# Chunked attention and a gated feed-forward: attention products in quarters of the array, two groups at a time

## The chip, the cores and the metric

The kernel runs on one core of one Trainium2 chip. A core has TensorE (PE in the profile, its weight loads PEld), VectorE (DVE), ScalarE (ACT), GpSimd (POOL, used here to issue loads that cast to bf16) and SyncE (SP, used here to issue transposing copies and the stores). The metric is the device time of one execution in microseconds. Before the change it is 248.89 us, the median of 3 runs (248.65 to 249.34).

## The reference, cut to what matters

q, k and v have 8 batches, 8 heads, 576 positions and 64 features, in float32. Attention stays within chunks of 64 positions, nine of them to a sequence. The result, 4608 tokens of 512 features, goes through a gated feed-forward.

```python
chunk = 64
q_c = q.reshape(B, H, nc, chunk, D)            # and k_c, v_c
scores = scale * np.matmul(q_c, k_c.transpose(0, 1, 2, 4, 3))
scores = scores - np.max(scores, axis=-1, keepdims=True)
attn = np.exp(scores)
attn = attn / (np.sum(attn, axis=-1, keepdims=True) + 1e-09)
out = np.matmul(attn, v_c).reshape(B, H, S, D)

x = out.transpose(0, 2, 1, 3).reshape(B * S, H * D)     # 4608 x 512
a, b = x @ w1, x @ w2                                   # 512 x 1024 each
h = a * b @ w3                                          # w3 1024 x 1024
return h @ w_out                                        # w_out 1024 x 512
```

## The kernel before, in words

**Groups and tiles.** A group is two chunks of all eight heads, 128 tokens; there are 36. Four groups make a tile of 512 tokens for the feed-forward, nine tiles in all. The kernel first forms w3 times w_out once (`add_w3o`: for each of eight rows of w3, 8 transposes, a copy, 8 products against w_out, a copy), so that a tile needs only `a` and `b` (64 products of 128x512, line 589), a multiplication `abT` on DVE (line 598), and 32 products against `w3o_sb` (line 620). `a` is copied out of PSUM by ACT first (`a_sb`).

**A group's attention** (`add_group`). q and k come as `raw` with tokens on the partitions. They are turned: groups 4 to 11 by PE (line 418, 8 transposes into a `ffn` buffer of PSUM, then copies), groups 12 to 35 by a transposing DMA on SP's queue into `kqT` (line 422). The scores of a pair of heads in one product need the two heads apart: q is copied into `qd`, a tile that is zero outside its two diagonal blocks (`q_copy`, two copies of 64 partitions), so that one product of full depth 128 and full width 128 gives 128x64 scores. Eight such products fill `p_sc` (line 447). Then DVE takes the maximum (line 452) and subtracts it (460), ACT takes the exponential (464), DVE sums, inverts and multiplies (468 to 474). The probabilities `an` are turned into `at`, for groups 0 to 15 by PE (line 479) and for the others by a DMA (line 428). Eight products against the padded v, `vd`, fill `p_av` (line 490); one copy takes that to `xt`, from which the feed-forward reads. `vd` and `qd` are zeroed at the start (lines 250 to 264).

**The first tile** is different: two "quads" (`load_quad`, `quad_turn`) bring q and k of four groups with rows of four tokens, 1 KB in DRAM, and PE turns 64 columns at a time, the two heads of a pair into the two halves of the partitions (line 380). Scores, values and copies undo the order of the tokens (lines 398, 405, 457).

**What sets the order.** Every step is added to a plan with the engines that it may run on, a cost, a key (the smaller the earlier), what it follows, and the buffers that it takes and reads. `Plan.run` plays this through and gives each engine a fixed order of instructions. Loads are issued by POOL in the order of the list `LOADS`, then group by group; the weights w1, w2, w3 and half of w_out, q, k and v all come by this one queue. The other half of w_out is staged by SP and ACT at the start (line 350). Stores start after the last load of q and k has come. Until the first product that takes `p_av`, PE's waits are filled with products on zeros (line 683).

**PSUM** has eight banks: six `ffn` buffers, one `p_sc`, one `p_av`. Scores hold theirs until DVE has subtracted the maximum, values until the copy to `xt` has been made.

Of the kernel before, what the change touches and what calls it, by code (L numbers as in the profile page):

```python
# [30 lines left out]
FLOWN, QUEUED, LAG = 3.5, 3.4, 1.2  # L31
# [143 lines left out]
def kernel(  # L175
# [21 lines left out]
    C = 64  # L197
# [16 lines left out]
    BUFS = {"raw": 6, "rawq": 2, "kqT": 4, "kT": 3, "qd": 3, "vd": 3, "sd": 2, "e": 2, "an": 4, "at": 6, "w3t": 2, "abT": 2,  # L214
            "a_sb": 3, "o_sb": 18, "xt": XT, "ffn": 6, "p_sc": 1, "p_av": 1}
# [19 lines left out]

    qds = [wpool.tile([P, 2, NM, 2 * C], bf, tag=f"qd{i}", name=f"qd{i}") for i in range(BUFS["qd"])]
    vds = [wpool.tile([P, NM, NCH, 2 * D], bf, tag=f"vd{i}", name=f"vd{i}") for i in range(BUFS["vd"])]
    rawqs = [wpool.tile([P, 2, 2, 2, R * D], bf, tag=f"rawq{i}", name=f"rawq{i}") for i in range(BUFS["rawq"])]
# [3 lines left out]
    plan = Plan(BUFS, ("qd", "kT", "kqT", "p_sc", "sd", "e", "an", "at", "p_av", "xt"))  # L242

    def copy(eng, o, i):
        if eng == "ACT":
            nc.scalar.copy(o, i)  # L246
        else:
            nc.vector.tensor_copy(o, i)  # L248

    zero_q = [plan.add("DVE", 0.5, -1000 + 2 * i, lambda eng, t=t: nc.vector.memset(t[:], 0.0))  # L250
              for i, t in enumerate(qds)]
    one_e = [plan.add("DVE", 0.1, -990, lambda eng, t=t: nc.vector.memset(t[:, :, C:], 1e-9)) for t in es]
    nought = consts.tile([P, 1], f32)
    zero_1 = plan.add("DVE", 0.1, -1002, lambda eng: nc.vector.memset(nought[:], 0.0))

    def zero(eng, t):
        if eng == "DVE":
            nc.vector.memset(t[:], 0.0)
        else:
            flat = t.rearrange("p m c d -> p (m c d)").bitcast(f32)  # L260
            nc.scalar.copy(flat, nought.to_broadcast(list(flat.shape)))

    zero_v = [plan.add(("DVE", "ACT", "ACT")[i], 2.0, (-999, -998, 9)[i], lambda eng, t=t: zero(eng, t), after=(zero_1,))
              for i, t in enumerate(vds)]


# [20 lines left out]
    quads, turned_in = {}, []  # L287

    def load_quad(n, y):
        box = quads[n, y] = {"ops": []}  # L290
        c0 = 8 * n
        cut = min(8, (c0 // NCH + 1) * NCH - c0)
        parts = [(c0, 0, cut)] + ([(c0, cut, 8)] if cut < 8 else [])
        for w, src in ((1, k), (0, q)):
            for t in range(2):
                for c, i0, i1 in parts:
                    def emit(eng, w=w, src=src, t=t, i0=i0, i1=i1):
                        if "t" not in box:
                            box["t"] = rawqs[len(turned_in) % len(rawqs)]
                            turned_in.append(box)  # L300
                        b, c = divmod(c0 + i0, NCH)
                        h = NM * t + 2 * y
                        nc.gpsimd.dma_start(box["t"][i0 * C // R:i1 * C // R, w, t],
                                            src[b, h:h + 2, c * C:(c + i1 - i0) * C, :].rearrange("h (p r) d -> p h (r d)", r=R))
                    box["ops"].append(load(0.084 * (i1 - i0), 0.5 + 0.02 * (i1 - i0), emit, takes=() if box["ops"] else ("rawq",)))

    def load_v(b, y0, y1):
        for t in range(2):
            def emit(eng, t=t):
                nc.gpsimd.dma_start(vds[b % len(vds)][halves[t], 2 * y0:2 * y1, :, t * D:(t + 1) * D].rearrange("p m c d -> p (m c) d"),  # L310
                                    v[b, NM * t + 2 * y0:NM * t + 2 * y1].rearrange("h (c p) d -> p (h c) d", p=C))
            o = load(1.07 * (y1 - y0), 0.5 + 0.335 * (y1 - y0), emit, takes=() if b in v_first else ("vd",),
                     after=(zero_v[b % len(vds)],))
            v_first.setdefault(b, o)
            for y in range(y0, y1):
                v_got.setdefault((b, y), []).append(o)

    def load_w12(j0, j1):
        for dst, w in ((w1_sb, moe_w1), (w2_sb, moe_w2)):
            for t in range(2):  # L320
                def emit(eng, dst=dst, w=w, t=t):
                    nc.gpsimd.dma_start(  # L322
                        dst[halves[t], :, j0 * P:j1 * P],
                        w[t * NM * D:(t + 1) * NM * D, j0 * P:j1 * P].rearrange("(m d) n -> d m n", d=D))
                o = load(0.342 * (j1 - j0), 0.62, emit)
        for j in range(j0, j1):
            w12_got[j] = o
# [34 lines left out]
    def add_group(g, kt, ks, ka, kv):  # L362
        box = {}
        quad = g < 4 * NQ
# [287 lines left out]
    for g in range(NG):  # L652
        if g >= 4 * NQ and g not in raws:
            load_qk(g)
# [61 lines left out]
```

## Time and profile before

| | |
|---|---|
| median of 3 runs | 248.89 us |
| profiled execution | 249.81 us |
| its span, first to last instruction | 248.0 us |
| PE busy | 239.6 us, 97% |
| DVE, ACT, POOL busy | 173.8, 146.3, 100.0 us |
| granted PE clock | 1.00 |

The page of the profile gives busy time for each engine, then the same in 40 slices of the span (6.2 us each), where a digit is tenths. The view of groups has, after the bar, the busy time, the mean length of one instruction in ns, and the idle time of the engine ahead of it with what ended most of it. The view of time gives start and length; a matmul's length there includes its way through the array, so the price of one in a dense row is the distance between starts, not the length. The chain of work follows from the last instruction back to what released each step.

### The profile page before, as it was taken

Reading aid. Unit: us, or ns where it says so; the run is one execution under the profiler, and the core shown is the slowest. Engines: PE = TensorE matmul, PEld = TensorE weight load, DVE = VectorE, ACT = ScalarE, POOL = GpSimd, SP = SyncE. Lnnn points to the kernel's source line nnn. Section 1 sums busy time; section 2 is a strip of 40 time slices with the busy share of each in tenths; the row PEclk is TensorE's granted clock in tenths of the full one; section 3 lists DMA queues with packets and bytes.
Section 4 is the critical chain, followed back from the end, with each engine's and each line's share of the span. In section 5 each row is a group of like instructions: output and inputs, shape, how many; then the busy total and the mean of one; then the engine's idle time right before and its main releaser. Section 6 shows DMA issues by size and latency. Waiting matters only on the chain.

```text
span 248.0 us, 4765 instructions
## 1 busy us (share of the span) xinstructions
PE 239.6 (97%) x1801; PEld 123.6 (50%) x1801; DVE 173.8 (70%) x315; ACT 146.3 (59%) x250; POOL 100.0 (40%) x127
## 2 busy tenths in 40 slices
PE   7699999899999999999999999999999999999994
PEld 2455665456555554545545455454454544444443
DVE  6287879768988878987887778868888862332310
ACT  8566756656876775576566655565677544323222
POOL 8755889969773482274227435400000000000000
PEclk9999999999999999999999999999999999999999
DMA  7999999999999999999999999999469994121114
GB/s 196 194 203 173 177 182 180 166 155 148 132 135 144 158 154 157 137 156 138 156 136 161 130 156 156 146 148 161 86 140 307 342 344 144 45 84 42 45 42 169
DMA packets 154310, 38.58 MB, mean 156 GB/s; under 512 B 141232, under 2 KB 148272, under 8 KB 154288
## 3 DMA queue, kind: packets, MB, share of 16 engines
q0 software_dynamic: 112016, 18.88, 104.0%
q1 hardware_dynamic: 41984, 18.88, 40.6%
q10 hardware_dynamic: 288, 0.52, 0.8%
q8 instruction: 14, 0.23, 0.4%
q14 instruction: 8, 0.07, 0.1%
HBM read 38.80 MB, written 9.44 MB: 194 GB/s over the span
## 4 chain that ended last, share of the span: by engine, by line
PE 79%; DMA 10%; POOL 7%; issue 1%; DVE 1%; ACT 1%; POOLq 0%
PE ffn L589 45%; PE ffn L620 25%; DMA vd<-in_v_dram 7%; POOL w_sb L322 4%; PE p_av L490 3%; PE p_sc L447 3%; DMA rawq<-in_k_dram 2%; POOL raw L284 2%; POOL vd L310 1%; PE ffn L479 1%; PE p_av L683 1%; PE ffn L418 1%; ACT w3t L246 0%; PE ffn L380 0%; DVE qd L248 0%
## 5 line engine op out<-in xcount | busy, mean ns | idle before, releaser
L589 PE MATMUL ffn<-xt,w_sb 128*128 128x512 bf16 x576 | 134.9, 379 | 0.0
L589 PEld LDWEIGHTS <-w_sb 128*128 128x128 bf16 x576 | 53.7, 98 | 57.6
L598 DVE TENSOR_TENSOR abT<-a_sb,ffn 128x512 bf16<-128x512 f32 x72 | 48.8, 682 | 35.0 <-PE ffn L589 33.9
L620 PE MATMUL ffn<-w3o_sb,abT 128*128 128x512 bf16 (+2 forms) x304 | 67.6, 368 | 0.0
L246 ACT COPY a_sb<-ffn 128x512 f32<-128x512 f32 x72 | 42.0, 585 | 35.6 <-PE ffn L589 35.3
L284 POOL DMA_DIRECT2D raw<-in_q_dram x36 | 30.6, 854 | 43.5 <-DMA kqT<-raw 25.6
L620 PEld LDWEIGHTS <-abT 128*128 128x128 bf16 x304 | 28.3, 98 | 30.1
L284 POOL DMA_DIRECT2D raw<-in_k_dram x36 | 30.8, 860 | 9.0 <-DMA vd<-in_v_dram 6.8
L468 DVE TENSOR_REDUCE ss<-e 128x8 f32<-128x520 bf16 x36 | 24.8, 689 | 4.5 <-ACT e L464 4.4
L452 DVE TENSOR_REDUCE nm<-p_sc 128x8 f32<-128x512 f32 x36 | 24.3, 676 | 4.7 <-PE p_sc L447 4.0
L464 ACT ACTIVATE e<-sd 128x512 bf16<-128x512 f32 x36 | 22.8, 634 | 4.6 <-DVE sd L460 3.5
L474 DVE TENSOR_TENSOR an<-e,rs 128x512 bf16<-128x512 bf16 x36 | 24.7, 685 | 0.4
L246 ACT COPY o_sb<-ffn 128x512 f32<-128x512 f32 (+2 forms) x18 | 9.7, 539 | 22.3 <-PE ffn L620 22.2
L246 ACT COPY qd<-kqT 64x512 bf16<-64x512 bf16 x36 | 22.1, 614 | 0.2
L460 DVE TENSOR_TENSOR sd<-p_sc,nm 128x512 f32<-128x512 f32 x32 | 21.8, 682 | 0.4
L246 ACT CAST xt<-p_av 128x512 bf16<-128x512 f32 x27 | 15.9, 588 | 9.1 <-PE p_av L490 7.3
L310 POOL DMA_DIRECT2D vd<-in_v_dram x16 | 18.6, 1173 | 1.7 <-DVE ss L468 1.0
L556 PE MATMUL ffn<-wo_sb,w3t 128*128 128x512 bf16 x64 | 15.7, 380 | 0.2
L490 PEld LDWEIGHTS <-vd 128*128 128x128 bf16 x256 | 11.4, 98 | 6.3 <-issue 0.6
L447 PEld LDWEIGHTS <-qd 128*128 128x128 bf16 x256 | 11.2, 98 | 5.7 <-ACT qd L246 0.5
L490 PE MATMUL p_av<-at,vd 128*128 128x64 bf16 x256 | 12.8, 193 | 0.5 <-DMA vd<-in_v_dram 0.5
L248 DVE CAST xt<-p_av 128x512 bf16<-128x512 f32 x9 | 6.2, 689 | 5.9 <-PE p_av L490 5.9
(53 smaller groups left out, 164.4 us busy)
## 6 DMA issues: line engine op xcount, KB each, us to landing
out_dram<-o_sb SPq DMA_DIRECT2D x19, 256.0 KB, 2.4
vd<-in_v_dram POOLq DMA_DIRECT2D x16, 288.0 KB, 12.1
raw<-in_q_dram POOLq DMA_DIRECT2D x28, 128.0 KB, 9.0
raw<-in_k_dram POOLq DMA_DIRECT2D x28, 128.0 KB, 8.6
w_sb<-in_moe_w_dram POOLq DMA_DIRECT2D x8, 256.0 KB, 8.3
w_sb<-in_moe_w_dram POOLq DMA_DIRECT2D x16, 128.0 KB, 5.4
out_dram<-w_sb SPq DMA_DIRECT2D x8, 256.0 KB, 4.5
out_dram<-wo_sb SPq DMA_DIRECT2D x4, 256.0 KB, 2.8
```

What stands on the lines that cost most here:

```text
L246: nc.scalar.copy(o, i)
L284: nc.gpsimd.dma_start(box["t"][r, w], src[b, :, c * C:(c + n) * C, :].rearrange("h p d -> p h d"))
L310: nc.gpsimd.dma_start(vds[b % len(vds)][halves[t], 2 * y0:2 * y1, :, t * D:(t + 1) * D].rearrange("p m c d -> p (m c) d"), v[b, NM * t + 2 ...
L452: nc.vector.tensor_reduce(nm[:, :, 0], box["sc"], axis=AX.X, op=ALU.max)
L460: nc.vector.tensor_sub(sd[:], box["sc"], box["nm"].to_broadcast([P, 8, C]))
L464: nc.scalar.activation(e[:, :, :C], box["sd"][:], ACT.Exp, scale=scale)
L468: nc.vector.reduce_sum(ss[:], box["e"][:], axis=AX.X)
L474: nc.vector.tensor_mul(an[:], box["e"][:, :, :C], box["rs"].to_broadcast([P, 8, C]))
L490: nc.tensor.matmul(t[:, m, cc, :], vds[b % len(vds)][:, m, c, :], box["at"][:, 2 * cc + y, u * C:(u + 1) * C], start=True, stop=True)
L589: nc.tensor.matmul(t[:, :w], wt[:, ki, j * P:(j + 1) * P], x[:, ki, :], start=(ki == 0), stop=(ki == KO - 1))
L598: nc.vector.tensor_mul(box["abT"][:, j, :w], box["as", j][:, :w], box["b", j][:, :w])
L620: nc.tensor.matmul(t[:, :x1 - x0], box["abT"][:, ki, tk * P:(tk + 1) * P], w3o_sb[:, ki, x0:x1], start=(ki == 0), stop=(ki == FO - 1))
```

## The change

Attention is computed for two groups at a time (`add_burst`; groups 0 to 3 one by one, `SINGLE = 4`). Scores: for each pair of heads and each chunk, the product of one head's q and k alone, 64 deep, 64 wide, 64 columns. The head decides on which half of the partitions q and k lie, the chunk to which half the result goes, so four products that follow each other lie in the four quarters of the array; the two heads write different banks. That is 16 products for a group and 32 for a pair, where there were 8 and 16. Values: the same, with the two chunks' positions on the halves of depth. q and k are used as they are turned, and v as it is loaded: `qd`, the padding of `vd`, their zeroing and the copies go. Where PE turns q and k (now groups 0 to 11), two copies of 128 partitions bring them to `kqT`.

Scores and values share one PSUM tile, `p_at`, of two banks and one buffer. Head h now stands on other partitions of x (the pairs are neighbours again), so w1 and w2 are loaded in plain order, in 8 loads of 128 partitions where there were 16 of 64; a product with w1 waits for its own load only. The first tile loses the quads and is loaded and turned like the others. The order of `LOADS` differs; one row of w3 (6) comes after the first parts of w1 and w2, and the first v after w3's rows 2, 5, 0, 4 and 7. There are more buffers of `kqT`, `at` and `o_sb`, a smaller key for the copies and multiplications of the feed-forward, and 14 products on zeros where there were 25.

```diff
-LOADS = [('quad', 0, 0), ('w3', 5, 6), ('w3', 6, 7), ('ident',), ('wo', 4, 8), ('w3', 1, 2), ('quad', 0, 1), ('w3', 4,
-         5), ('w3', 0, 1), ('w3', 2, 3), ('v', 0, 0, 2), ('qk', 4), ('w3', 7, 8), ('w3', 3, 4), ('qk', 6), ('qk', 5),
-         ('w12', 0, 2), ('w12', 2, 4), ('w12', 6, 8), ('qk', 7), ('w12', 4, 6), ('v', 1, 0, 2), ('qk', 8), ('qk', 9),
-         ('qk', 10)]
+LOADS = [('qk', 0), ('qk', 1), ('w3', 2, 3), ('ident',), ('qk', 2), ('w3', 5, 6), ('wo', 4, 8), ('qk', 3), ('w3', 0,
+         1), ('w3', 4, 5), ('qk', 4), ('w3', 7, 8), ('v', 0, 0, 2), ('w3', 1, 2), ('w3', 3, 4), ('qk', 6), ('qk', 5),
+         ('w12', 0, 2), ('w12', 6, 8), ('qk', 7), ('w12', 4, 6), ('qk', 8), ('w3', 6, 7), ('w12', 2, 4), ('qk', 9),
+         ('v', 1, 0, 2), ('qk', 10)]
-NQ = 1
+SINGLE = 4
-FLOWN, QUEUED, LAG = 3.5, 3.4, 1.2
+FLOWN, QUEUED, LAG = 3.0, 3.4, 1.2
...
-    BUFS = {"raw": 6, "rawq": 2, "kqT": 4, "kT": 3, "qd": 3, "vd": 3, "sd": 2, "e": 2, "an": 4, "at": 6, "w3t": 2, "abT": 2,
-            "a_sb": 3, "o_sb": 18, "xt": XT, "ffn": 6, "p_sc": 1, "p_av": 1}
+    BUFS = {"raw": 6, "kqT": 6, "vd": 3, "sd": 2, "e": 2, "an": 4, "at": 8, "w3t": 2, "abT": 2,
+            "a_sb": 3, "o_sb": 24, "xt": XT, "ffn": 6, "p_at": 1}
...
-    vds = [wpool.tile([P, NM, NCH, 2 * D], bf, tag=f"vd{i}", name=f"vd{i}") for i in range(BUFS["vd"])]
+    vds = [wpool.tile([P, NM, NCH, D], bf, tag=f"vd{i}", name=f"vd{i}") for i in range(BUFS["vd"])]
...
+        def s_emit(eng):
+            sc = ps("p_at", [P, 2, 2, 4, C])
+            for i in range(len(gs)):
+                kq = boxes[i]["kq"]
+                boxes[i]["sc"] = sc[:, :, i]
+                for y in range(2):
+                    for t in range(2):
+                        for u in range(2):
+                            for cc in range(2):
+                                x = kq[halves[u], :, y + 2 * t, cc * C:(cc + 1) * C]
+                                nc.tensor.matmul(sc[halves[cc], u, i, 2 * y + t, :], x[:, 0], x[:, 1], start=True, stop=True)
+
+        def av_emit(eng):
+            av = ps("p_at", [P, 2, 2, 2, 2, C])
+            for i in range(len(gs)):
+                boxes[i]["av"] = av[:, :, i]
+                for y in range(2):
+                    for cc, (b, c) in enumerate(chunks(gs[i])):
+                        for t in range(2):
+                            for u in range(2):
+                                nc.tensor.matmul(av[halves[u], t, i, y, cc, :], vds[b % len(vds)][halves[t], 2 * y + u, c, :],
+                                                 boxes[i]["at"][halves[t], 2 * u + y, cc * C:(cc + 1) * C], start=True, stop=True)
...
+        cost = 0.2 + 0.11 * len(gs)
+        s = plan.add("PE", cost, keys[0][1], s_emit, after=kq_done, takes=("p_at",), uses=kq_used, lag=0.2)
...
+        av = plan.add("PE", cost, keys[0][3], av_emit, after=box["av_after"], takes=("p_at",), uses=box["av_uses"], lag=0.2)
...
-            c = plan.add("ACT", 0.18 + 0.11 * n, kab(j) - 1, a_copy, after=(a,), takes=("a_sb",), uses=[(a, "ffn")])
-            muls.append(plan.add("DVE", 0.18 + 0.13 * n, kab(j) - 1, mul, after=(b, c), uses=[(b, "ffn"), (c, "a_sb")]))
+            c = plan.add("ACT", 0.18 + 0.11 * n, kab(j) - 20, a_copy, after=(a,), takes=("a_sb",), uses=[(a, "ffn")])
+            muls.append(plan.add("DVE", 0.18 + 0.13 * n, kab(j) - 20, mul, after=(b, c), uses=[(b, "ffn"), (c, "a_sb")]))
...
-    for g in range(NG):
+    for gs in [(g,) for g in range(SINGLE)] + [(g, g + 1) for g in range(SINGLE, NG, 2)]:
+        keys = []
+        for g in gs:
             late = min(LATE if g < TURN_A else LATE_A, g // 2)
-        add_group(g, *(3 * g - n + late for n in AHEAD[:1] * (g in QK_BY_DMA) + AHEAD[1 + (g in QK_BY_DMA):]))
+            dma = g in QK_BY_DMA
+            keys.append([3 * g - x + late for x in AHEAD[:1] * dma + AHEAD[1 + dma:]])
+        add_burst(gs, keys)
```

More of the change, by code (lines that the diff above doesn't have):

```diff
@@ L517, in add_group, with at_turn @@
[L517 to L520 removed]
+        def at_turn(eng):
+            at = box["at"] = sb("at", [P, 4, P])
+            nc.sync.dma_start_transpose(at[:], box["an"].rearrange("p x k -> p (x k)"))
@@ L674 @@
         nc.vector.memset(zeros[:], 0.0)
-        warm = ps("p_av", [P, TT])
+        warm = ps("p_at", [P, 2, TT])[:, 0]
         fills, last, cold = 14, 0.0, True
@@ L678 @@
             if o.engine == "PE":
-                cold = cold and "p_av" not in o.takes
+                cold = cold and "p_at" not in o.takes
                 if last:
```

231 lines of the change are left out of this document (66 added, 165 removed).

## The prediction

> **What bounds the kernel now.** I read the page first, then the chain of work that ended last, then the order of time on PE around the first feed-forward product, then the groups.
>
> ```profile
> span 248.0 us, 4765 instructions
> PE 239.6 (97%) x1801; PEld 123.6 (50%) x1801; DVE 173.8 (70%) x315; ACT 146.3 (59%) x250; POOL 100.0 (40%) x127
> PE   7699999899999999999999999999999999999994
> DMA  7999999999999999999999999999469994121114
> ```
>
> PE is the bound almost from the start: its slices read 9 from the third on. DVE and ACT have room. The DMA engines are busy too, up to slice 28, so early on loads decide what PE can be given.
>
> The chain, in order of time (start, length, what):
>
> ```profile
> 17.30 9.31 DMA vd<-in_v_dram
> ...
> 54.63 0.45 PE ffn L418 x8
> 55.08 0.23 PE p_av L490 x8
> ...
> 114.34 3.45 PE ffn L589 x16
> ```
>
> Unit prices on a dense PE: a 128x512 product is 3.45/16 = 0.216 us, a 128x128 transpose 0.45/8 = 0.056 us, and eight padded attention products take 0.23 us, 0.029 us each. The first v is complete at 17.30 + 9.31 = 26.6 us.
>
> PE in order of time:
>
> ```profile
> 36.86 1.03 PE L589 MATMUL ffn<-xt,w_sb 128*128 128x512 bf16 x4
> ...
> 42.95 1.03 PE L589 MATMUL ffn<-xt,w_sb 128*128 128x512 bf16 x4
> 44.69 0.62 PE L418 MATMUL ffn<-ident,raw 128*128 128x128 bf16 x8 [0.72 <-DMA raw<-in_k_dram]
> 45.15 1.89 PE L589 MATMUL ffn<-xt,w_sb 128*128 128x512 bf16 x8
> 47.05 0.41 PE L447 MATMUL p_sc<-kT,qd 128*128 128x64 bf16 x8
> ...
> 51.84 0.28 PE L490 MATMUL p_av<-at,vd 128*128 128x64 bf16 x4
> 52.63 0.28 PE L490 MATMUL p_av<-at,vd 128*128 128x64 bf16 x4 [0.51 <-DMA vd<-in_v_dram]
> ```
>
> Feed-forward work starts at 36.86. After it PE waits three times: 42.95 + 4 x 0.216 = 43.81 to 44.69, 0.88; 46.88 to 47.05, 0.17; 51.96 to 52.63, 0.67. Together 1.7 us; I found no further pause of PE before its last product. So the end is: start of the feed-forward work, plus the PE work that is left then, plus 1.7, plus the last output's way out. The change is worth what it does to these four.
>
> **The attention products.** Before, a group costs two bursts of eight products of 128x64, 0.23 us each. Now a burst is 16 products of 64x64 for a group, 32 for a pair: twice as many, meant to run four at a time in the four quarters of the array. No row shows quarters, but one line of before uses halves: the quad's transposes write 64 columns, two halves in turn.
>
> ```profile
> 17.06 0.61 PE L545 MATMUL ffn<-ident,w_sb 128*128 128x128 bf16 x8
> 17.60 0.64 PE L380 MATMUL ffn<-ident,rawq 128*64 128x128 bf16 x16
> 18.17 0.40 PE L479 MATMUL ffn<-ident,an 128*128 128x128 bf16 x4
> ...
> L380 PE MATMUL ffn<-ident,rawq x64: 219/219/243, 7.3 to 20.2; 128*64 128x128 bf16 x64
> ```
>
> (The last row is the view of one tile: shortest, median, longest in ns.) From 17.06 to 18.17 is 1.11 us. The eight whole transposes are 0.45. If the 16 half ones ran one by one at 0.056 they alone would take 0.89, so they overlap in twos: 8 x 0.056 = 0.45. What is left, 1.11 - 0.90 = 0.21 to 0.22, is the price of going into the divided array and back. The Trainium skill, "TensorEngine Tiling (Array Packing)", Key Properties, says that a change of tiling mode drains TensorE; the 0.22 us agrees, and the page has no price.
>
> For quarters the price lies between these ends. Best: all four overlap, 32 products as 8 steps of 0.029 = 0.23 us, and the switch hidden. Worst: nothing overlaps, 32 x 0.029 = 0.93 plus 0.22. I take full overlap with the whole switch, 0.23 + 0.22 = 0.45 for a pair and 0.12 + 0.22 = 0.34 for a single group, since the half-array row shows both the overlap and the price. Before, the same pair cost 2 x 0.23 = 0.46, so pairs are level; a single group loses 0.11 a burst, but the four single groups lie ahead of the feed-forward work, where PE waits for loads anyway. In the order of PE's instructions, what follows the first feed-forward product was 31 score bursts and 32 value bursts, 63 x 0.23 = 14.5 us, and is now 16 + 16 pairs, 32 x 0.45 = 14.4. Change: 0.0 (the 0.1 is rounding).
>
> A rule of the Trainium skill speaks against the edit: "TensorEngine Tiling (Array Packing)", Instruction Overhead, gives each small product some 60 cycles whatever its size and warns against tiling a dimension that is already small; "TensorE: Matmul & The Clock Gate", Back-to-back issue gap, puts that floor at about 25 ns. Paid by all 32 products in turn it would be, as an estimate from these pages, 0.8 us a burst against 0.23. The half-array row speaks against it so far, with 36 ns a transpose where 56 is the price of a whole one.
>
> Heads in another place on x, and the rows of w1 and w2 with them, change no size: 0.
>
> **Copies that go.**
>
> ```profile
> L246 ACT COPY qd<-kqT 64x512 bf16<-64x512 bf16 x36 | 22.1, 614 | 0.2
> L248 DVE COPY qd<-kqT 64x512 bf16<-64x512 bf16 x12 | 3.8, 315 | 0.3
> L261 ACT COPY vd<-nought 128x2304 f32<-128x2304 f32 x2 | 4.1, 2108 | 0.0
> ...
> ACT a_sb L246 <- PE ffn L589: 35.3, 55, 1.7
> DVE abT L598 <- PE ffn L589: 33.9, 30, 3.0
> ```
>
> The 48 copies from kqT into the padded q, 22.1 + 3.8 = 25.9 us, and the zeroing of v, 4.1 us on ACT, leave, and so do the memsets and eleven of the products on zeros that fill PE's early waits. On the path they are worth 0: both engines already wait some 35 us each for the feed-forward products of PE. If that cover were gone, they would be a gain, not a cost.
>
> **One PSUM tile for scores and values.** p_sc and p_av, a buffer each, become one p_at of two banks, so every attention burst waits until the one before it is read out.
>
> ```profile
> L452 DVE TENSOR_REDUCE nm<-p_sc 128x8 f32<-128x512 f32 x36 | 24.3, 676 | 4.7 <-PE p_sc L447 4.0 <-PE p_sc L398 0.6
> L460 DVE TENSOR_TENSOR sd<-p_sc,nm 128x512 f32<-128x512 f32 x32 | 21.8, 682 | 0.4
> L248 DVE CAST xt<-p_av 128x512 bf16<-128x512 f32 x9 | 6.2, 689 | 5.9 <-PE p_av L490 5.9
> ```
>
> After a pair of scores DVE needs 2 x 0.676 + 2 x 0.682 = 2.7 us; after a pair of values ACT and DVE side by side need 0.7. In the new order the other PE work between is at least 3.45 us after scores (16 products) and 1.73 after values (8), mostly 4 to 8. Covered; I take 0. If DVE came one multiply (0.68) late at each of the twelve narrowest turns, it would cost 12 x 0.68 = 8.2.
>
> **First tile in plain form, and the loads.** Two quads (eight loads of q and k) become four groups of two loads each, with short rows.
>
> ```profile
> 10.00:20.00 10.00, 9.19 (x110) 5.28 (x110) 7.77 (x15) 6.27 (x10) 5.88 (x9) 1.00 1.22 197
> 15.00:17.00 2.00, 2.00 (x11) 0.88 (x9) 1.97 (x5) 0.60 (x2) 0.96 (x2) 1.00 1.44 193
> 53.00:57.00 4.00, 4.00 (x36) 2.26 (x35) 2.31 (x5) 2.19 (x4) 4.00 (x5) 1.00 2.41 158
> ```
>
> The last number is GB/s: 193 while quads land, 158 while plain q and k land, 197 among w3. A load writes 131 KB: 0.68 us as quad, 0.83 plain; a w3 row (262 KB) 1.33. Ahead of the first v there were 8 quad loads, six w3 rows and w_out; now 10 plain loads (five groups), five w3 rows and w_out: 8.3 - 5.4 - 1.3 = +1.6, so v comes at 26.6 + 1.6 = 28.2. Behind it in POOL's queue come w3 rows 1 and 3 (29.6, 30.9), groups 6 and 5 (32.5, 34.2) and the first quarter of w1 (35.5). PE's order from there: values of group 0, w3 row 1 turned at 29.6, values of group 1 at 30.0, row 3 turned at 30.9, 0.86 of products, values of group 2, group 6 turned 32.5 to 33.0, 0.86, values 0.34, 0.86, group 5 turned 0.45, 0.86: feed-forward starts at 36.4, 0.5 earlier than 36.86. If plain loads ran at the quads' rate v would come 1.5 sooner; if a microsecond later, all of it moves along.
>
> But one row of w3 (row 6) is now loaded after the first weights, so its 8 transposes and 8 products, 0.45 + 1.73 = 2.2 us of PE work that before lay in the load-bound stretch, now stand behind the start. That is a loss of 2.2. Both forms leave five groups to be turned by PE and twelve probability transposes after the start: level.
>
> The pauses after the start: the wait for the second v (0.67) goes, as the pair 4, 5 now multiplies 23 us of PE work after the start, at 60 us, and its v is due near 55 us by the same rates. The one for group 7 (0.88) I halve: its load is due at 41.6 where PE's order reaches it near 42. 1.7 becomes about 0.9: -0.8. w1 and w2 in 8 loads instead of 16 carry the same bytes; POOL saves issues, and POOL is ahead anyway.
>
> Sum on the span: 248.0 - 0.5 + 2.2 + 0.0 - 0.8 = 248.9. The profiled execution took 249.8 for a span of 248.0, and the median of the three runs is 248.89, span plus 0.9. Predicted: 248.9 + 0.9 = **249.8**.
>
> **Rivals.**
> - Slower, the quarters do not run four at a time. If only halves overlap, a pair is 16 x 0.029 + 0.22 = 0.68, and 32 x 0.23 = 7.4: 257. If nothing does, 0.93 + 0.22 = 1.15, 32 x 0.70 = 22: 272. If each step also shows its weight load, which for halves showed only in the first product (243 against 219 ns), 8 x 0.024 x 32 = 6: 256. For: the steps are half as long as those that hid it. Against: two halves did overlap. Chance 0.16.
> - Slower, p_at's turns make PE wait, about a third of the 8.2: 252.5. For: every turn now passes DVE. Against: DVE waits for PE, as quoted. Chance 0.13.
> - Faster, the switch costs half of 0.22, since a quarter's products have only 64 rows to drain: 32 x 0.11 = -3.5, so 246.3. It decides from a switch below 0.17 us, where the 1.7 us down to the faster bound are made up. For: the 0.22 was measured on 128 rows. Against: a switch goes both ways, and one side is always the whole array. Chance 0.17.
> - No change to speak of: loads come 1.5 us sooner than I add up, 248.3. Chance 0.13.
> - The forecast, with a range of its own of 248.4 to 251.2 for half a microsecond or so of error in each of its terms: chance 0.41.
>
> **How the numbers follow.** A change under 0.3%, 0.75 us, cannot be told from none here: same is 248.1 to 249.6. Of the forecast 0.11 falls there and 0.30 above; of the load case 0.08 is same and 0.05 faster; the switch case is faster, the two others slower. Faster 0.22, same 0.19, slower 0.59. The range runs from the switch case to the one with the weight load, 246.3 to 256.0, and leaves out the other two cases of the quarters, about 0.12.
>
> **What would show it.** Starts of 64x64 products in fours, about 0.03 us from four to four; 0.22 us around each burst; w3 row 6 turned after the first feed-forward product; that product near 36.4; PE waits after it under 1 us, none of them before an attention burst; the copies into qd gone and ACT and DVE idle longer. Wrong if a burst of 32 takes 0.6 us or more, if PE waits at p_at, or if the first v comes later than 29.

## The result, and the profile after

The changed kernel takes 251.46 us (median of 4 runs, 251.20 to 251.52). The kernel before, run beside it, took 249.12 (248.65 to 249.56). The ratio is 1.0088, with a 95% interval of 1.0067 to 1.0110: slower by 2.2 us. The forecast was 249.8, slower, with a range of 246.3 to 256.0. (The two medians differ by 2.3.) The sign and the range hold, the size of the loss was forecast at less than half.

The page of the changed kernel begins with these lines:

```profile
span 249.2 us, 5756 instructions
PE 237.7 (95%) x2334; PEld 115.4 (46%) x2334; DVE 161.7 (65%) x288; ACT 121.8 (49%) x210; POOL 97.4 (39%) x119
PE   7486999999999999999999999999999999999994
DMA  8999999999999999999999999999399995121114
```

DVE is 12 us less busy than before and ACT 24.5 us, as the copies are gone. PE still reads 9 from the fifth slice on. Its first slices read 7, 4, 8, 6 where the kernel before had 7, 6, 9, 9: the plain first tile keeps PE waiting more at the start.

PE in order of time around the start of the feed-forward (start, length, line, count):

```profile
34.18 1.04 PE L470 MATMUL ffn<-wo_sb,w3t 128*128 128x512 bf16 x4
35.06 0.61 PE L330 MATMUL ffn<-ident,raw 128*128 128x128 bf16 x8
...
36.37 1.03 PE L502 MATMUL ffn<-xt,w_sb 128*128 128x512 bf16 x4
37.32 0.45 PE L357 MATMUL p_at<-kqT 64*64 64x64 bf16 x32
37.70 4.49 PE L502 MATMUL ffn<-xt,w_sb 128*128 128x512 bf16 x20
...
48.16 0.61 PE L459 MATMUL ffn<-ident,w_sb 128*128 128x128 bf16 x8
...
53.60 1.89 PE L470 MATMUL ffn<-wo_sb,w3t 128*128 128x512 bf16 x8
55.42 0.45 PE L357 MATMUL p_at<-kqT 64*64 64x64 bf16 x32
55.80 0.40 PE L425 MATMUL ffn<-ident,an 128*128 128x128 bf16 x4
56.03 1.89 PE L533 MATMUL ffn<-w3o_sb,abT 128*128 128x512 bf16 x8
```

The feed-forward starts at 36.37. Row 6 of w3 is turned at 48.16 and multiplied at 53.60, behind the start. Each burst of a pair takes 0.47 us: 37.70 less 36.37 + 4 x 0.216.

The whole course of PE can be put into five numbers: when the feed-forward starts; the other PE work behind that (each 128x512 product at 0.216, each transpose at 0.056); the attention bursts; the waits between; and what follows after the last product has begun. I worked them out from the starts of all matmuls in each trace, in us:

| | start | work | bursts | waits | after | span |
|---|---|---|---|---|---|---|
| before, as profiled above | 36.9 | 191.4 | 14.7 | 1.7 | 3.4 | 248.0 |
| before, profiled again | 36.9 | 191.4 | 14.7 | 2.6 | 3.3 | 248.9 |
| changed | 36.4 | 193.6 | 15.4 | 0.5 | 3.4 | 249.2 |

(Bursts of the changed kernel: 32 x 0.47, and 0.01 us by which the product behind each burst holds up its successor.) So the changed kernel starts 0.5 earlier, has 2.2 more work, 0.7 more in the bursts and 1.2 less in waits than the first profile of before. The 0.5 us of waits is one place, at 105 us, in the view of waits of PE:

```profile
PE ffn L502 <- ACT xt L244: 0.4, 1, 0.4
```

### The profile page after: what moved, and what is told of

Same layout as the page of the kernel before. It is cut to its first block, busy times and chain, and to the rows that moved or that the text cites. A ratio compares the mean times of both kernels' runs of the same rounds, so it can differ in the third digit from the quotient of the medians.

```text
span 249.2 us, 5756 instructions
## 1 busy us (share of the span) xinstructions
PE 237.7 (95%) x2334; PEld 115.4 (46%) x2334; DVE 161.7 (65%) x288; ACT 121.8 (49%) x210; POOL 97.4 (39%) x119
## 4 chain that ended last, share of the span: by engine, by line
PE 89%; DMA 4%; POOL 4%; ACT 1%; issue 0%; DVE 0%; ACTq 0%; POOLq 0%
PE ffn L502 51%; PE ffn L533 25%; DMA w_sb<-in_moe_w_dram 4%; PE ffn L470 4%; PE p_at L367 3%; POOL raw L266 3%; PE p_at L357 3%; PE ffn L330 2%; PE ffn L425 1%; PE ffn L459 1%; POOL w_sb L289 1%; ACT w3t L244 0%; POOL wo_sb L296 0%; DVE xt L246 0%; ACT a_sb L244 0%
## 5 line engine op out<-in xcount | busy, mean ns | idle before, releaser
L533 PE MATMUL ffn<-w3o_sb,abT 128*128 128x512 bf16 (+2 forms) x304 | 67.3, 368 | 0.0
L266 POOL DMA_DIRECT2D raw<-in_q_dram x40 | 34.3, 861 | 35.0 <-DMA kqT<-raw 20.0
L533 PEld LDWEIGHTS <-abT 128*128 128x128 bf16 x304 | 28.6, 98 | 31.4
L244 ACT COPY o_sb<-ffn 128x512 f32<-128x512 f32 (+2 forms) x25 | 13.8, 552 | 35.9 <-PE ffn L533 35.7
L401 DVE TENSOR_REDUCE nm<-p_at 128x8 f32<-128x512 f32 x36 | 23.6, 685 | 8.2 <-PE p_at L357 8.1
L420 DVE TENSOR_TENSOR an<-e,rs 128x512 bf16<-128x512 bf16 x36 | 24.5, 684 | 0.2
L405 DVE TENSOR_TENSOR sd<-p_at,nm 128x512 f32<-128x512 f32 x36 | 24.0, 680 | 0.0
L246 DVE CAST xt<-p_at 128x512 bf16<-128x512 f32 x15 | 10.4, 692 | 10.3 <-PE p_at L367 8.1
L244 ACT CAST xt<-p_at 128x512 bf16<-128x512 f32 x21 | 12.0, 590 | 6.4 <-DVE xt L246 3.2
L244 ACT COPY kqT<-ffn 128x512 bf16<-128x512 bf16 x19 | 10.6, 587 | 6.1 <-PE ffn L330 4.1
L357 PEld LDWEIGHTS <-kqT 64*64 64x64 bf16 x576 | 6.2, 108 | 8.9 <-issue 6.8
L367 PEld LDWEIGHTS <-vd 64*64 64x64 bf16 x576 | 6.3, 108 | 8.4 <-issue 4.9
L357 PE MATMUL p_at<-kqT 64*64 64x64 bf16 x576 | 8.4, 196 | 1.5 <-ACT kqT L244 1.5
## 6 DMA issues: line engine op xcount, KB each, us to landing
out_dram<-o_sb SPq DMA_DIRECT2D x23, 256.0 KB, 2.3
w_sb<-in_moe_w_dram POOLq DMA_DIRECT2D x16, 256.0 KB, 8.4
out_dram<-w_sb SPq DMA_DIRECT2D x8, 256.0 KB, 3.1
out_dram<-wo_sb SPq DMA_DIRECT2D x4, 256.0 KB, 3.8
o_sb<-in_moe_w_out_dram ACTq DMA_DIRECT2D x2, 256.0 KB, 4.4
```

The source lines that it names most:

```text
L266: nc.gpsimd.dma_start(box["t"][r, w], src[b, :, c * C:(c + n) * C, :].rearrange("h p d -> p h d"))
L357: nc.tensor.matmul(sc[halves[cc], u, i, 2 * y + t, :], x[:, 0], x[:, 1], start=True, stop=True)
L401: nc.vector.tensor_reduce(nm.rearrange("p (u x) o -> p u (x o)", u=2), box["sc"], axis=AX.X, op=ALU.max)
L405: nc.vector.tensor_sub(sd.rearrange("p (u x) k -> p u x k", u=2), box["sc"], box["nm"].to_broadcast([P, 8, C]).rearrange("p (u x) k -> p u ...
L420: nc.vector.tensor_mul(an[:], box["e"][:, :, :C], box["rs"].to_broadcast([P, 8, C]))
L533: nc.tensor.matmul(t[:, :x1 - x0], box["abT"][:, ki, tk * P:(tk + 1) * P], w3o_sb[:, ki, x0:x1], start=(ki == 0), stop=(ki == FO - 1))
```

## The experiments

Every ratio is to the kernel before, run on the same occasion. Its medians were 249.12 to 249.60 from one occasion to the next, and the changed kernel was run on the first alone, so a difference to its 251.46 us is uncertain by some 0.5 us.

**The kernel before again.** Nothing is changed. The question is whether the 1.7 us of waits, and the profiled execution's 249.81, were typical.

> The kernel before, unchanged, profiled once more. The profiled execution on which the prediction rests took 249.8 us while the median of the plain runs was 249.1, and its PE waited 1.7 us in three places after the feed-forward work had begun (0.88 for q and k of a late group, 0.17, and 0.67 for the second v). Theory A (those waits were a chance of that one execution): the new profile shows clearly less of them, under 1 us in sum, and a span near 247. Theory B (they belong to the kernel): 1.5 to 1.9 us of waits at the same places and a span of 248.

Measured: 249.33 us (248.54 to 250.63, 10 runs), ratio 0.9999 (0.9971 to 1.0027). The new profiled execution took 250.63 for a span of 248.9. The view of waits (us in total, times, longest) puts the difference into one place. In the first profile of before it has this row:

```profile
PE ffn L418 <- DMA raw<-in_k_dram: 0.7, 1, 0.7
```

In the second profile the same row reads:

```profile
PE ffn L418 <- DMA raw<-in_k_dram: 1.7, 1, 1.7
```

The load of group 7 landed 1 us later (45.66 us, before 44.65), and the execution was 0.8 us longer. So the places of the waits are those of theory B, but in these two profiles their size differs, and the time with it. The ten executions spread over 2 us; that all of it comes from such waits is not shown. In every execution of before whose span is on record, time and span differ by 1.72 to 1.85 us.

**The first tile.** First the kernel before with a plain first tile: groups 0 to 3 are loaded like the others, at the places of the quads in the list, and no other line of the program differs. The planner makes another order from this list, so the order of all engines is part of what is compared.

```diff
-LOADS = [('quad', 0, 0), ('w3', 5, 6), ('w3', 6, 7), ('ident',), ('wo', 4, 8), ('w3', 1, 2), ('quad', 0, 1), ('w3', 4,
+LOADS = [('qk', 0), ('qk', 1), ('w3', 5, 6), ('w3', 6, 7), ('ident',), ('wo', 4, 8), ('w3', 1, 2), ('qk', 2), ('qk', 3), ('w3', 4,
...
-NQ = 1
+NQ = 0
```

> The kernel before with one part of the change: the two quads in the list of loads are replaced in their places by the plain loads of groups 0 and 1, and 2 and 3; attention stays in padded products of the whole array. Theory A (the loss of the change sits in the loads of the first tile): eight plain loads at 0.83 us for eight at 0.68, so the first v and all behind it come 1.2 us later, and the time is about 250.3, near the changed kernel's 251.4 or beyond it. Theory B (the loss sits in the quarter products, their switches and the shared PSUM tile): no change, 249.1.

Measured: 253.67 us (252.92 to 254.24, 4 runs), ratio 1.0179 (1.0150 to 1.0207), 4.3 us slower and more than either theory had. The feed-forward starts at 38.3, 1.5 later, and waits behind it are 3.6 us. The view of waits of PE names what is late:

```profile
PE ffn L418 <- DMA raw<-in_k_dram: 3.2, 5, 1.7
PE p_sc L447 <- ACT qd L246: 2.6, 4, 1.0
```

The second row is the point: PE waits 2.6 us for ACT's copies into the padded q, at four places. Two of them, 1.5 us together, lie far behind the start:

```profile
73.48 0.39 PE L447 MATMUL p_sc<-kqT,qd 128*128 128x64 bf16 x8 [0.96 <-ACT qd L246]
83.52 0.41 PE L447 MATMUL p_sc<-kqT,qd 128*128 128x64 bf16 x8 [0.50 <-ACT qd L246]
```

In the kernel before, PE waits 0.6 us for a copy into `qd` ahead of the start. Behind it, the smallest of the three waits in the prediction (0.17 us) is of this kind too, as the weight load of that product shows:

```profile
47.05 0.29 PEld L447 LDWEIGHTS <-qd 128*128 128x128 bf16 x8 [0.51 <-ACT qd L246]
```

Then the other way: the changed kernel with the first tile in quads and the list of loads of before.

```diff
-LOADS = [('qk', 0), ('qk', 1), ('w3', 2, 3), ('ident',), ('qk', 2), ('w3', 5, 6), ('wo', 4, 8), ('qk', 3), ('w3', 0,
+LOADS = [('quad', 0, 0), ('w3', 5, 6), ('w3', 6, 7), ('ident',), ('wo', 4, 8), ('w3', 1, 2), ('quad', 0, 1), ('w3', 4,
...
+NQ = 1
...
+            if g < 4 * NQ:
+                raw = quads[g // 4, g % 4 // 2]
```

> The changed kernel with one part undone: the first tile is loaded and turned in the quads' form again, with the list of loads of before; its attention runs in quarters like the rest. The subtraction of the maximum is two instructions instead of one in the four groups of that tile. Theory A (loss in the loads of the first tile): the time returns nearly to that of before, 249.1 plus 0.4 for 32 bursts at 0.470 us against 63 at 0.2325, so 249.5. Theory B (loss in the quarter products and the shared PSUM tile): it stays at 251.4.

Measured: 252.30 us (252.07 to 252.55, 4 runs), ratio 1.0126 (1.0105 to 1.0147). Neither theory. The start is 0.5 earlier (35.8) and work behind it 1.3 less, but 3.6 us of waits stand in the new order, on the probabilities, on `p_at` and on `raw` among others. So the plain first tile can't be priced by itself: with the padded copies the kernel with it is 4.3 us slower, and without them it is not slower than the one with quads. In both pairs the order differs too, and how much of each difference is the order's is not shown.

**Row 6 of w3.** The first try left the PE work of row 6 out and let ACT fill its rows by a copy of other data. The planner then made another order.

```diff
+        if ko == 6:
+            w3o_done.append(plan.add("ACT", 0.7, key, lambda eng: copy(eng, w3o_sb[:, ko, :], w3_sb[:, ko, :D_MODEL]), after=(w3_got[ko],)))
+            return
```

> The changed kernel without PE's work on row 6 of w3 (8 transposes and 8 products, 2.18 us); a copy by ACT stands in its place, so the product of w3 and w_out is left out for that row, and all loads stay. Theory A (the row, moved behind the start of the feed-forward work, costs its whole length there): 251.4 - 2.2 = 249.2. Rival (the row fills a stretch in which PE would wait for the last part of w1 and w2 anyway): 251.4, with waits of PE in place of the row.

Measured: 251.77 us (251.67 to 252.57, 4 runs), ratio 1.0103 (1.0079 to 1.0126). The 2.2 us of work went, and start (+0.8) and waits (+2.6) took their place. As the order had changed everywhere, this told little, so the second try kept the order and cut only the contents of row 6.

```diff
-            for ki in range(FO):
+            for ki in range(FO) if ko != THIN else wo_cut[0][:1]:
                 nc.tensor.transpose(t[:, ki, :], w3_sb[:, ko, ki * P:(ki + 1) * P], ident[:])
...
-                for ki in range(*wo_cut[i]):
+                for ki in range(*wo_cut[i]) if ko != THIN else wo_cut[0][:1 - i]:
```

> The order of every engine is that of the changed kernel; row 6 of w3 alone is cut down to one transpose, a copy of one block and one product, so that its rows of the product of w3 and w_out are incomplete. That takes 7 x 0.056 + 7 x 0.216 = 1.9 us of PE work from behind the start of the feed-forward and moves nothing else. Theory A (the move of row 6 behind the start is what costs): 251.46 - 1.9 = 249.55 us, ratio to before 1.001. Theory B (PE is held there by loads or by DVE in any case, so that the work only fills a wait that comes back): 251.2 to 251.5, ratio 1.008.

Measured: 251.02 us (250.48 to 251.61, 10 runs), ratio 1.0058 (1.0036 to 1.0080): 0.4 us less than the changed kernel (0.7 by the ratios) where the work that went is 1.9. PE in order of time shows why:

```profile
53.77 0.38 PE L473 MATMUL ffn<-wo_sb,w3t 128*128 128x512 bf16 x1
54.08 0.32 PE L358 MATMUL p_at<-kqT 64*64 64x64 bf16 x16
54.56 0.32 PE L358 MATMUL p_at<-kqT 64*64 64x64 bf16 x16 [0.17 <-ACT kqT L245]
55.73 0.40 PE L426 MATMUL ffn<-ident,an 128*128 128x128 bf16 x4 [0.84 <-DVE an L421]
55.96 1.89 PE L536 MATMUL ffn<-w3o_sb,abT 128*128 128x512 bf16 x8
```

Seven of the eight products of row 6 are gone at 53.77, and PE waits for a copy of ACT and for the probabilities of DVE instead. It reaches the next feed-forward product (L536 here, L533 in the changed kernel) at 55.96 where the changed kernel does at 56.03. In this stretch PE is held by DVE, which is busy 4.86 of 5 us from 52 to 57 (4.01 in the changed kernel):

```profile
52.00:57.00 5.00, 3.98 (x60) 2.30 (x59) 4.86 (x10) 3.15 (x6) 3.29 (x4) 1.00 2.43 159
```

(Stretch, its length, then busy time and instructions of PE, weight loads, DVE, ACT, POOL, and granted clock, DMA engines, GB/s.) Theory B holds for the larger part. The start, 36.9, was 0.5 later in this profile, where the clock had been lower before it (below); without that the gain might be 0.9, which is still half of the 1.9. One execution of each kernel ran at a mean clock of 1.00: their spans are 248.5 and 249.2, a gain of 0.7.

**Quarters of the array.** Four kernels ask what a burst costs. First, each product is issued twice:

```diff
-            for i in range(len(gs)):
+            for i in [i for i in range(len(gs)) for _ in range(2)]:
```

> Every product of a burst is issued twice, with the same operands and result, so that a burst of a pair has 64 products in place of 32; the order of all else is that of the changed kernel. Theory A (a fixed 0.22 us for going into the quarters and back, and 0.029 us for each four products): 0.22 + 2 x 0.24 = 0.71 us a burst, 32 x 0.24 = 7.8 us more behind the start, 259.3. Theory B (no fixed part, 0.015 us for each product): 0.94 us a burst, 15 us more, 266.5. Theory C (the products are hidden behind the switch): 0.47 a burst, 251.4.

Then no pairs, every group for itself:

```diff
-SINGLE = 4
+SINGLE = 36
```

> Every group by itself, as the first four are, in place of two at a time: 64 bursts of 16 products stand behind the start where there were 32 of 32. Theory A (each way into the quarters and back has its fixed price): a burst of 16 in 4 steps of 0.031 us and 0.22 us, 0.34 in all, 64 x 0.34 = 21.8 where the pairs took 32 x 0.47 = 15.0, so 6.8 us more, 258. Theory B (0.015 us for each product and nothing fixed): 0.24 a burst, 251.4.

The order within a burst, quarter by quarter, so that four products (of one group) of the same quarter stand in a row:

```diff
-                for y in range(2):
-                    for t in range(2):
-                        for u in range(2):
-                            for cc in range(2):
+                for u in range(2):
+                    for cc in range(2):
+                        for y in range(2):
+                            for t in range(2):
```

> Only the order of the products within a burst differs: all of one quarter of the array stand in a row, then those of the next, where the changed kernel goes round the four quarters. Theory A (quarters run side by side only because neighbours in the order lie in different quarters, and a switch of 0.22 us is paid once for each burst): up to 0.22 + 32 x 0.029 = 1.15 us a burst, 32 bursts x 0.68 = 22 us more, 273. Theory B (each product of 64 x 64 costs 0.47/32 = 0.015 us wherever it lies): 251.4, bursts of 0.47.

And both together, twice each and 16 of one quarter in a row:

> Every product of a burst is issued twice, and all those of one quarter stand in a row, 16 of them, then the next quarter's. To be read against the kernel that issues each product twice and goes round the quarters (a burst of 0.73 us). Theory A (PE runs quarters side by side only as far ahead as a few products reach; four in a row were still within that, 16 are not): quarters mostly one after the other, 64 x 0.029 us and 0.22, up to 2.1 us a burst, and 30 us and more on the time. Theory B (the price is what PE needs to begin a load and a product, 0.008 to 0.010 us, wherever they lie): 0.22 + 64 x 0.0093 = 0.81 us a burst, the time within 3 us of the kernel with each product twice.

The view of time on PE, one burst of each; the price is the start of the row behind the burst less the start of the row ahead of it and 0.216 for each of its products. The changed kernel, 0.47:

```profile
96.87 1.03 PE L502 MATMUL ffn<-xt,w_sb 128*128 128x512 bf16 x4
97.83 0.45 PE L357 MATMUL p_at<-kqT 64*64 64x64 bf16 x32
98.20 0.40 PE L425 MATMUL ffn<-ident,an 128*128 128x128 bf16 x4
```

Each product twice, 0.74:

```profile
105.71 1.03 PE L502 MATMUL ffn<-xt,w_sb 128*128 128x512 bf16 x4
106.67 0.71 PE L357 MATMUL p_at<-kqT 64*64 64x64 bf16 x64
107.31 0.40 PE L425 MATMUL ffn<-ident,an 128*128 128x128 bf16 x4
```

Single groups, 0.35:

```profile
102.06 1.90 PE L502 MATMUL ffn<-xt,w_sb 128*128 128x512 bf16 x8
103.89 0.32 PE L357 MATMUL p_at<-kqT 64*64 64x64 bf16 x16
104.14 1.04 PE L502 MATMUL ffn<-xt,w_sb 128*128 128x512 bf16 x4
```

Four of a quarter in a row, 0.51:

```profile
97.99 1.03 PE L502 MATMUL ffn<-xt,w_sb 128*128 128x512 bf16 x4
98.94 0.49 PE L357 MATMUL p_at<-kqT 64*64 64x64 bf16 x32
99.36 0.40 PE L425 MATMUL ffn<-ident,an 128*128 128x128 bf16 x4
```

Sixteen of a quarter in a row, each product twice, 1.94:

```profile
102.62 1.03 PE L504 MATMUL ffn<-xt,w_sb 128*128 128x512 bf16 x4
103.58 1.91 PE L358 MATMUL p_at<-kqT 64*64 64x64 bf16 x64
105.42 0.40 PE L427 MATMUL ffn<-ident,an 128*128 128x128 bf16 x4
```

16, 32 and 64 products cost 0.35, 0.47 and 0.74 us. That is a straight line to within 0.02 us: 0.22 us fixed, and 0.032 us for every four, or 0.008 each. The fixed part is the way in and out; the four quarters do run side by side, as padded products in a row took 0.029 each. With 16 of one quarter in a row the same 64 products take 1.94 - 0.22 = 1.72, or 0.027 each, so then they run nearly one by one. With four in a row 0.04 us is lost and no more: the overlap reaches over four, though not over 16. (In the kernel with 16 a product is also repeated 4 products later, where the one with 0.74 us repeats it 16 later; that this costs nothing was not tried.)

The times: single groups 258.84 us (ratio 1.0393), as theory A had it, so taking two groups at a time is worth 7.4 us. Four in a row 253.48 (1.0155), near theory B: 32 x 0.04 = 1.3 us of the 2.0 are bursts. Sixteen in a row 303.51 (1.2186), theory A. Each product twice 266.05 (1.0658): the bursts are 32 x 0.27 = 8.6 longer, as theory A had it, but the time is nearly 7 us above its 259.3. The view of time on PE has the place:

```profile
67.75 0.51 PE L357 MATMUL p_at<-kqT 64*64 64x64 bf16 x40
71.39 0.53 PE L357 MATMUL p_at<-kqT 64*64 64x64 bf16 x24 [3.13 <-issue]
```

In the middle of a burst PE stands still for 3.1 us and no semaphore or buffer is named. From 71 to 75 us the granted clock is then 0.57. The pause and 4 us at that clock make some 5 of the 7 us. What it waited for is not shown; this program has 2300 more PE instructions, and its instruction queue moved 27 packets where that of the changed kernel moved 18, which fits a late fetch of instructions but doesn't prove it.

**The copies that went.** Their work is put back as dummies, from a tile of zeros to a tile that nobody reads, at fixed places in the order of the changed kernel.

```diff
+            if g < 12:
+                nc.vector.tensor_copy(spare2[halves[1]], nought[halves[1]])
             nm = box["nm"] = sb("nm", [P, 8, 1], f32, bufs=3)
...
+            nc.scalar.copy(spare[halves[1]], nought[halves[1]])
             e = box["e"] = es[g % len(es)]
```

> The changed kernel with the work of the removed copies put back as dummies: one copy of 64x512 on ACT ahead of each exponential (36), and one on DVE ahead of each maximum of groups 0 to 11 (12), from a tile of zeros to a tile that nobody reads. The order of all else stays. Theory A (the prediction: copies off PE's path are worth nothing): 251.2 to 251.7, ratio 1.009. Theory B (while the first tiles are worked on, from 40 to 57 us, DVE and ACT are what PE waits for, so the copies that went did pay there): 0.6 us for each of the one to four places, 252 to 254, ratio 1.012 to 1.02.

Measured: 255.70 us (254.93 to 256.30, 4 runs), ratio 1.0265 (1.0233 to 1.0297): 4.2 us over the changed kernel, more than theory B. The feed-forward starts at 39.4, 3.0 later, and waits behind it rise from 0.5 to 2.6. The loads came as in the changed kernel (the first v landed at 27.99 with the dummies and at 28.04 in the changed kernel), so the late start is not theirs. The view by stretches ahead of the start (stretch, length, busy time of PE, weight loads, DVE, ACT, POOL, granted clock):

```profile
14.00:18.00 4.00, 3.32 (x24) 2.42 (x23) 2.98 (x7) 1.84 (x3) 1.50 (x3) 0.50 1.72 184
18.00:22.00 4.00, 4.00 (x27) 1.40 (x26) 2.81 (x6) 1.26 (x3) 2.75 (x4) 0.57 1.65 185
```

PE ran this stretch at half the clock and was busy all the time from 18 to 22, where the changed kernel had full clock and 2.11 of 4 us busy. How much of the 3.0 us is the copies' directly, and how much a clock that fell longer because PE waited for them, these rows can't part; a shorter fall went with 0.4 to 0.6 us in other runs (below). Of the other executions, one ran at a mean clock of 0.993 with a span of 253.0, where one of the changed kernel at 0.993 had 249.5: 3.5 us at the same mean clock. The 2.1 us of waits behind the start, at full clock, are the copies'. The view of waits has them in two rows:

```profile
PE ffn L506 <- ACT xt L244: 1.0, 3, 0.4
PE ffn L429 <- DVE an L424: 0.6, 3, 0.3
```

Those for `an` stand at 59 to 67 us, those for `xt` at 110, 138 and 184, so they are not confined to the first tiles as theory B had it. A planner that knew of the copies might have placed them better. So 4.2 is an upper figure for this order, but 0 is wrong.

**Fewer ways in and out.** If each way costs 0.22 us, scores of one pair and values of another should share one. Scores and values get two banks each, the feed-forward four.

```diff
+        if len(gs) == 2 and len(held) == HOLD:
+            prev = held.pop(0)
+
+            def both(eng):
+                prev["emit"](eng)
+                s_emit(eng)
```

> The scores of one pair and the values of the pair two before it are issued as one burst of 64 products, so that 14 of the 32 ways into the quarters and back after the start go. For that, scores and values have a PSUM tile of two banks each, the feed-forward four banks in place of six, raw four buffers and kqT eight. Theory A (the way in and out costs 0.22 us each time and PE is the bound): 14 x 0.22 = 3.1 us less, 248.3, ratio 0.997. Theory B (with four banks PE waits for ACT and DVE to empty them, or a joint burst waits for the later of its two inputs): what is won is lost in waits, 251 or more, ratio 1.007 and above.

Measured: 250.41 us (249.79 to 250.86, 10 runs), ratio 1.0030 (1.0008 to 1.0051). The switches went as expected: 17 bursts behind the start, 14 of them joint at 0.74 to 0.79 us (without the waits inside two of them), take about 12 us where 32 took 15.4. But waits rise from 0.5 to about 3 us, among them three of 0.5 for the copy to `xt`: a pair's two copies to `xt`, put on ACT and DVE by the plan, ran one after the other.

Last, this together with the quads, and an order of loads in which all of w3 comes ahead of w1 and w2:

```diff
+LOADS = [('w3', 6, 7), ('w3', 0, 1), ('w3', 2, 3), ('ident',), ('wo', 4, 8), ('quad', 0, 0), ('w3', 5, 6), ('quad', 0, 1), ('w3', 7, 8), ('qk', 4), ('w3', 4, 5), ('v', 0, 0, 2), ('w3', 1, 2), ('w3', 3, 4), ('qk', 5), ('qk', 6), ('w12', 0, 1),
...
+NQ = 1
+LATE, LATE_A = -4, -1
+AHEAD = [29.0, 26.0, 22.5, 17.5, 20.0]
```

> An attempt at a kernel that is faster than both: scores and values of two pairs in one burst, the first tile in quads as before the change, and another order of loads in which all of w3 comes ahead of w1 and w2, so that no row of w3 is multiplied behind the start. Theory A (the work of PE behind the start and the switches set the time): before's work of 191.4, bursts of 12.2 where before had 14.7, a start of 36 to 37, and waits as before: 247 to 248.5, ratio 0.993. Theory B (what is taken off PE comes back as waits, as in the other orders tried): waits of 4 us or more, 249.5 to 252, ratio 1.0 to 1.01.

Measured: 249.53 us (248.78 to 249.92, 10 runs), ratio 1.0013 (1.0000 to 1.0026). That is 0.8% under the changed kernel and level with the kernel before. Work is 191.4 and bursts 12, as theory A had them, but the start is 37.7 and waits are 3 us, the largest of 1.1 on a load of k and of 0.9 on `xt`: they eat the gain. So theory B holds for the time, with 3 us of waits where it had 4. No kernel of this study is faster than the one before.

## Why the prediction was right or wrong

**The start, right.** Forecast 36.4, measured 36.37; v was due at 28.2 and landed at 28.04, rows 1 and 3 of w3 at 29.6 and 30.9 and landed at 29.24 and 30.49. That is one profile, at full clock; with the clock falls described below the same order started 0.4 to 0.6 later.

**The quarters, right in kind, 0.7 us short in size.** All four run at once and the whole way in and out is paid, as the quad's transposes had shown. Priced at 0.45, a burst is 0.47, and 0.01 more for the product behind it: 15.4 us, where before had 14.7. The rivals of the quarters and of the switch at half price fall with the straight line above. The Trainium skill, "TensorEngine Tiling (Array Packing)", Instruction Overhead, gives each small product some 60 cycles whatever its size; the traces differ: 0.008 us a product, where the prediction's estimate from that rule was 0.025.

**Row 6 and the pauses, right as a sum, wrong as two things.** The work is 2.2 us as forecast, and the waits fell by 1.2 where 0.8 was forecast. But they are one matter: with the row cut away in an unchanged order, 1.3 us of waits came back in its place and the time fell by 0.4. The row fills time in which PE would wait for DVE and ACT. The step took every microsecond of PE work behind the start as a microsecond of time, and PE, though its slices read 9, is not the only bound until about 56 us.

**The copies, wrong.** "On the path they are worth 0" was read from DVE's and ACT's idle time over the whole span. Stage by stage the room is not always there. In the changed kernel DVE is busy 3.97 of 4 us from 48 to 52 (columns as above):

```profile
48.00:52.00 4.00, 4.00 (x26) 2.06 (x25) 3.97 (x9) 2.73 (x5) 3.17 (x5) 1.00 2.42 161
```

Put back, the copies cost between 2.1 and 4.2 us, and in the kernel before with a plain first tile PE waits 2.6 us for them. From the kernel before to the changed one little of this shows: with quads, PE waits for a copy into `qd` 0.2 us behind the start and no more, and the kernel with a plain first tile and the padded copies is 4.3 us slower. So the removal of the copies seems to pay for the plain first tile. The prediction priced neither the copies nor the waits for them, and that its sum came near the span all the same is in part luck; that the two cancel is argued from kernels with orders of their own, not measured.

**p_at, right here.** In the changed kernel no attention burst behind the start waits at `p_at`. Other orders had such waits: in the one without row 6 the view has 0.7 us at 65 us and 0.3 at 199.

**Fewer products on zeros, costed at nothing, not quite so.** See the clock below: a fall of the clock went with half a microsecond in some profiles of this order; in that of the changed kernel there was none.

**The step that failed is the last one, "248.9 + 0.9".** The span was forecast at 248.9 and measured at 249.2 (bursts +0.7, waits -0.4). But the 0.9 set the span of a profiled execution against the median of three others that were faster. In each single execution the time is the span plus 1.8 before, and plus 2.0 after. The right sum is 249.2 + 2.0 = 251.2, the profiled execution's time. The median of four is 0.3 above that: the three other executions had spans of 249.5, at mean clocks of 0.984 to 0.993 where the profiled one had 1.00. So of the 1.7 us between 249.8 and 251.46, 0.3 lie in the span, 1.1 in the 0.9 that should have been 2.0, and 0.3 in the execution that was profiled. The prediction may also have taken off one thing twice: the wait for group 7 is what differs between the two profiles of before, and it left both as a pause and with the faster median; no faster execution was profiled, so this isn't shown. The kernel before, run some 45 times more beside the experiments, had medians of 249.25 to 249.6, so 248.89 was itself a low draw. Why 0.2 us more lie outside the span after the change stays open. The measured 251.46 lies just above the forecast's own 248.4 to 251.2; the wider range holds it because it reached up to a rival's 256.0, and that rival, a weight load shown in each step (0.64 us a burst), is not what happened.

## What to carry to other kernels

Take off or add work on an engine by the stage, not by its idle time over the span: copies that seem covered may hold the start, and PE work that seems costly may only fill a wait. Form the sum on spans, and add what a single execution has beside its own span; a median of other runs is another quantity. Work that goes into quarters of the array paid about 0.22 us here each time it went in and out, so it is gathered into few long bursts that go round the quarters.

## What the runs showed of the hardware

**How far ahead quarters overlap.** Sixteen products of one quarter in a row lose the overlap (0.027 us a product in place of 0.008, in bursts of 64), four in a row keep nearly all of it (0.51 us a burst of 32 in place of 0.47).

**In this order the clock falls at the start, in most executions.** The kernel with row 6 cut has the order of the changed kernel and the same loads, and yet ran the stretch from 11 to 14 us at half the clock. The view by stretches (columns as for the copies), for the changed kernel:

```profile
8.00:11.00 3.00, 1.73 (x39) 1.28 (x36) 1.53 (x3) 1.19 (x3) 3.00 (x5) 1.00 1.86 176
11.00:14.00 3.00, 2.49 (x38) 1.50 (x36) 2.95 (x7) 1.55 (x3) 2.66 (x5) 1.00 1.40 202
```

And for the kernel with row 6 cut, with 0.80 and 0.50 in the column of the clock:

```profile
8.00:11.00 3.00, 1.72 (x31) 1.17 (x28) 1.51 (x3) 0.65 (x2) 3.00 (x5) 0.80 1.80 172
11.00:14.00 3.00, 2.35 (x27) 1.48 (x28) 2.00 (x4) 1.54 (x3) 2.31 (x4) 0.50 1.44 200
```

Five of six profiles with the changed kernel's order show such a fall between 8 and 22 us; neither profile of before does. The mean clock of every execution agrees: it was 0.978 to 0.993 in 22 of 24 executions of these six kernels, and 0.998 or more in all 55 of the kernel before that have it on record. The profile of the changed kernel shows one of the two without a fall. In three of the five profiles, which have little or nothing more to do ahead of the start, the feed-forward starts 0.4 to 0.6 later; that the clock is the cause is likely, not shown. PE is idle for most of the stretch from 6 to 10 us now (busy 1.13 of 4), which the kernel before filled with seven products on zeros; whether such products here would hold the clock was not tried. The Trainium skill, "TensorE: Matmul & The Clock Gate", Part 1: The HAM clock gate, says that the gate halves the clock after an idle window of about 3.4 us that runs freely of the kernel; that one order falls in some executions and not in others agrees with it, and the length of the window no run here shows.
